# Reordering the first key chunks and splitting the query weight load at the start of a fused attention and feed-forward kernel

## The chip, the cores and the metric

The kernel runs on one core of one Trainium2 chip. The metric is device time in microseconds (us), and each number quoted for a kernel is the median of several runs. A profile's span is 1.2 to 1.4 us shorter than the time of the same run.

PE is TensorE's matmul, PEld its weight load, DVE is VectorE, ACT is ScalarE, and SP is SyncE, which here only issues transfers. ACT issues transfers too. "SPq" and "ACTq" are their issuing sequencers.

## The reference, cut to what matters

```python
def reference(A_x, A_wqkv, A_wo, B_x, B_w_gate, B_w_up, B_w_down, gate_w):
    x = A_x                                             # (1, 2048, 640), bf16
    g = sigmoid((x * gate_w).sum(-1, keepdims=True))
    # linear attention: q, k, v = x @ wqkv (640 -> 3 x 640), phi(q), phi(k), then @ wo
    a = _A_ref(x, A_wqkv, A_wo)
    b = (gelu(x @ w_gate) * (x @ w_up)) @ w_down        # 640 -> 1728 -> 640
    return g * a + (1 - g) * b
```

Only the start matters here: the key and query projections of the first two tiles of 128 rows of x. The contraction has length 640, so each projection is a sum of five chunks of 128 (k = 0 to 4).

Of the kernel before, what the change touches and what calls it, by code (L numbers as in the profile page):

```python
# [16 lines left out]
KC = D // 128  # L17
# [144 lines left out]
def bass_gated_mix__linear_attn_block__geglu_ffn__prompt_kernel(  # L162
# [63 lines left out]
    with (  # L226
# [8 lines left out]
        with contextlib.ExitStack() as stack:  # L235
# [12 lines left out]
            def new_dma_key():  # L248
                k = "in%d" % dma_next[0]
                dma_next[0] += 1  # L250
                return k
# [17 lines left out]
            wq = wkq[:, :, 640:1281]  # L269
# [40 lines left out]
            r_wq = [P.sb("wq%d" % k, R_WK + k * WW + 640, R_WK + k * WW + 1280) for k in range(KC)]  # L310
# [28 lines left out]
            def dma_in(dst, src, writes, reads=(), eng="sp"):  # L339
                P.op(eng, lambda e, dst=dst, src=src: e.dma_start(dst, src),  # L340
                     reads=reads, writes=writes, dma=new_dma_key())
# [6 lines left out]
            def load_wk(k, eng="sp"):  # L348
                dma_in(wk[:, k, :], A_wqkv[k * 128:(k + 1) * 128, 640:1280], [r_wk[k]], eng=eng)

            def load_wq(k0, k1, eng="sp"):
                dma_in(wq[:, k0:k1, 0:640],
                       A_wqkv[k0 * 128:k1 * 128, 0:640].rearrange("(k p) w -> p k w", p=128),
                       r_wq[k0:k1], eng=eng)


            P.op("act", lambda e: e.dma_start(touch[0:16, 0:4], A_wqkv[0:128:8, 640:644]),
# [10 lines left out]
            load_wk(4, "act")  # L368
            P.op("dve", lambda e: e.memset(gw_sb, 0.0), writes=[r_gw])
            dma_in(gw_sb[0:5, :], gate_w.rearrange("(k p) -> k p", p=128), [r_gw], eng="act")  # L370
            load_wq(0, 2)
            load_wq(2, KC, "act")

            def load_xT(i, after=()):
                P.op("sp", lambda e: e.dma_start_transpose(xT[:, :, i * 128:(i + 1) * 128],
# [50 lines left out]
            def slot(n):  # L426
                return SLOTS[n % 4]
# [17 lines left out]
            def KM(n, ks):  # L445
                i = seq[n][1]
                b0, b1 = slot(n)

                def fn(e):
                    last = None  # L450
                    for k in ks:
                        lhs = xT[:, k, i * 128:(i + 1) * 128]
                        e.matmul(ps[:, b0, :], lhs, wk[:, k, 0:512], start=(k == 0), stop=(k == KC - 1))  # L453
                        last = e.matmul(ps[:, b1, 0:128], lhs, wk[:, k, 512:640],
                                        start=(k == 0), stop=(k == KC - 1))
                    return last
                P.op("pe", fn, reads=[r_xTa[i] if i < NXN and ks == [0] else r_xT[i]] + [r_wk[k] for k in ks],
                     writes=[bank[b0], bank[b1]])

            def QM(n, ks):  # L460
                i = seq[n][1]
                b0, b1 = slot(n)

                def fn(e):
                    last = None
                    for k in ks:
                        lhs = xT[:, k, i * 128:(i + 1) * 128]
                        e.matmul(ps[:, b0, :], lhs, wq[:, k, 0:512], start=(k == 0), stop=(k == KC - 1))  # L468
                        last = e.matmul(ps[:, b1, 0:129], lhs, wq[:, k, 512:641],  # L469
                                        start=(k == 0), stop=(k == KC - 1))  # L470
                    return last
                P.op("pe", fn, reads=[r_xT[i], r_gcol] + [r_wq[k] for k in ks],
                     writes=[bank[b0], bank[b1]])

            def phi1(n):
                b0, b1 = slot(n)
                m = n % 4
                P.op("act", lambda e: e.activation(e_buf[m], ps_flat[:, b0 * 512:b0 * 512 + 640], ACT.Exp),
                     reads=[bank[b0], bank[b1]], writes=[r_e[m]])
                kind, i = seq[n]  # L480
                if kind == "q":
                    P.op("act", lambda e: e.activation(eg[:, i:i + 1], ps[:, b1, 128:129], ACT.Tanh, scale=0.5),
                         reads=[bank[b1]], writes=[r_eg[i]])

            def phi2(n):
                b0, b1 = slot(n)
                m = n % 4
                P.op("dve", lambda e: e.tensor_scalar(e_buf[m], e_buf[m], 1.0, EPS, ALU.min, ALU.add),
                     reads=[r_e[m]], writes=[r_e[m]])
                kind, i = seq[n]  # L490
                dst, r_dst = (pk[i], r_pk[i]) if kind == "k" else (pq[i], r_pq[i])
                P.op("dve", lambda e: e.scalar_tensor_tensor(
                    dst, ps_flat[:, b0 * 512:b0 * 512 + 640], 1.0 + EPS, e_buf[m], ALU.add, ALU.max),
                    reads=[bank[b0], bank[b1], r_e[m]], writes=[r_dst])

            def gate_col():

                P.op("pe", lambda e: e.matmul(ps[:, 7, 0:5], gw_sb, ident[:, 0:5], start=True, stop=True),
                     reads=[r_gw, r_ident], writes=[bank[7]])
                P.op("dve", lambda e: e.tensor_copy(wq[:, :, 640:641], ps[:, 7, 0:5].unsqueeze(2)),  # L500
                     reads=[bank[7]], writes=[r_gcol])
# [10 lines left out]
            T(1, [1, 2, 3, 4], 6)  # L512
            warm(3, 128)
            KM(1, [0])
            for k in (1, 3):
                KM(0, [k])
                KM(1, [k])
            gate_col()
            for k in (2, 4):
                KM(0, [k])  # L520
                KM(1, [k])
            for n in range(4):
                if n == 2:
                    for k in range(3):
                        QM(2, [k])
                        QM(3, [k])
                    QM(2, [3, 4])
                    QM(3, [3, 4])
                phi1(n)
                phi2(n)  # L530

# [398 lines left out]
```

## The kernel before: the parts that the change touches

The weights are loaded in pieces from two engines' queues. `dma_in(..., eng=...)` issues one load; whoever reads a piece waits for that load's own semaphore (a counter that the load's 16 shares raise one by one as they land: in the trace of this kernel those of key chunk 3 landed from 5.51 to 6.96 us, and the matmul that waited for it started at 7.01).

```python
load_x(0)                        # SP:  x tile 0, 160 KB
load_wk(0)                       # SP:  key weights, chunk 0, 160 KB
load_x(1, "act")                 # ACT: x tile 1
load_wk(1)
load_wk(3)                       # SP:  third key chunk on this queue
# [cut: one tiny activation]
load_wk(2, "act")
load_wk(4, "act")
# [cut: the gate vector, 1.2 KB, on ACT]
load_wq(0, 2)                    # SP:  query weights, chunks 0 and 1, one load of 320 KB
load_wq(2, KC, "act")            # ACT: query weights, chunks 2 to 4, one load of 480 KB
# [cut: 14 transposing loads of the other x tiles, which wait for key chunk 4; all later weights]
```

Tiles 0 and 1 are transposed on TensorE (`T`), with filler matmuls (`warm`) in the pauses. `KM(n, [k])` multiplies key chunk k of tile n (a matmul of 512 and one of 128 columns), `QM` does the same for queries (512 and 129 columns). `seq[2]` and `seq[3]` are the queries of tiles 0 and 1.

```python
warm(5, 512); warm(1, 128)
T(0, [0], 7); T(0, [1, 2, 3, 4], 6)
warm(6, 128)
KM(0, [0])
T(1, [0], 7); T(1, [1, 2, 3, 4], 6)
warm(3, 128)
KM(1, [0])
for k in (1, 3):
    KM(0, [k]); KM(1, [k])
gate_col()                       # one matmul of 5 columns
for k in (2, 4):
    KM(0, [k]); KM(1, [k])
for n in range(4):
    if n == 2:
        for k in range(3):
            QM(2, [k]); QM(3, [k])
        QM(2, [3, 4])
        QM(3, [3, 4])
    phi1(n); phi2(n)             # exponential on ACT, min and max on DVE
for i in range(2, NT):           # every other tile: keys and queries together, "joint tiles"
    KQ(i)                        # 15 matmuls, 2.7 us
```

After the joint tiles come the key-value products and the feed-forward block, another 220 us of matmuls.

## Time and profile before

| | before |
|---|---|
| time, median of 3 | 274.45 us (274.27 to 275.06) |
| span of the profile | 273.2 us |
| PE busy | 269.7 us (99%) |
| first key matmul | 4.62 us |
| first query matmul | 8.67 us |
| first joint tile | 11.40 us |

From the page of the kernel before, the span, the busy time of the engines, and the chain of work that ended last by engine:

```profile
span 273.2 us, 3449 instructions
PE 269.7 (99%) x1369; PEld 128.6 (47%) x1369; DVE 141.9 (52%) x251; ACT 76.0 (28%) x132; POOL 30.0 (11%) x28
...
PE 97%; DMA 2%; SPq 0%; DVE 0%; issue 0%
```

TensorE is nearly always busy and the chain is made of it. The list of PE's waits, for the whole run (engine, line, what it waited for, us in total, times, longest):

```profile
PE ps L419 <- PEq L915: 0.8, 1, 0.8
PE ps L453 <- DMA pool<-in_A_wqkv_dram: 0.8, 2, 0.6
```

So PE's only waits are the launch and 0.8 us for key weights (L453 is the key matmul). The chain in order of time (start, us, what) shows which load that was:

```profile
2.17 0.04 issue
2.21 4.76 DMA pool<-in_A_wqkv_dram
6.96 0.05 issue
7.01 0.39 PE ps L453
```

The load issued third on SP's queue, key chunk 3, ends at 6.96 and the next key matmul starts at 7.01. The timeline of PE (start, us, engine, line, operation, count, and the wait before it if one is listed) shows the gap; L453 and L454 are keys, L468 queries, L540 the joint tiles:

```profile
4.62 0.38 PE L453 MATMUL ps<-pool 128*128 128x512 bf16 x1 [0.18 <-DMA pool<-in_A_wqkv_dram]
...
6.20 0.22 PE L454 MATMUL ps<-pool 128*128 128x128 bf16 x1
7.01 0.39 PE L453 MATMUL ps<-pool 128*128 128x512 bf16 x1 [0.59 <-DMA pool<-in_A_wqkv_dram]
...
8.67 0.38 PE L468 MATMUL ps<-pool 128*128 128x512 bf16 x1
...
11.40 0.81 PE L540 MATMUL ps<-pool 128*128 128x512 bf16 x3
```

The listed time of a matmul is longer than the step to the next one: 0.38 us is listed for 512 columns and 0.22 for 128, but the next matmul starts 0.22 us after one of 512 columns and 0.05 after one of 128. From the start at 6.20 the next should have come at 6.26, so the gap is 0.75 us. The page's transfer list gives the two query loads: 320 KB took 5.9 us from issue to landing, 480 KB took 6.1. Issued at 2.68 and 3.32, they landed at about 8.5 and 9.4.

### The profile page before, as it was taken

The numbers are of one execution on the slowest core, as the hardware profiler recorded it, in microseconds if no ns is written. First come the engines' busy times: TensorE is split into PE (matmuls) and PEld (weight loads), VectorE is DVE, ScalarE is ACT, GpSimd is POOL, SyncE is SP. The second block draws the span as 40 slices with busy tenths as digits, with TensorE's granted clock in tenths as the row PEclk, the third lists the DMA queues.
The fourth block names the chain that finished last, engine by engine and source line by source line (L and its number), as shares of the span: only waits on it lengthen the run. The fifth ranks groups of instructions, "written<-read, shape, count | busy, mean of one in ns | idle before, by whom it ended". The sixth has DMA issues, their size and how long they took to land.

```text
span 273.2 us, 3449 instructions
## 1 busy us (share of the span) xinstructions
PE 269.7 (99%) x1369; PEld 128.6 (47%) x1369; DVE 141.9 (52%) x251; ACT 76.0 (28%) x132; POOL 30.0 (11%) x28
## 2 busy tenths in 40 slices
PE   7999999999999999999999999999999999999997
PEld 4555555544445444444444444444444444444444
DVE  2588989998234334999999999634210000000200
ACT  2355555310421454223222223224011121121021
POOL 5000000003240001242332422000000000000000
PEclk9999999999999999999999999999999999999999
DMA  6675999500300011522121221263031110110211
GB/s 207 179 118 122 322 402 386 143 3 12 65 19 2 23 49 51 182 45 48 26 48 24 48 42 34 60 215 109 5 77 38 41 38 19 38 41 19 58 58 41
DMA packets 42160, 23.61 MB, mean 86 GB/s; under 512 B 31519, under 2 KB 40735, under 8 KB 42015
## 3 DMA queue, kind: packets, MB, share of 16 engines
q1 hardware_dynamic: 41269, 22.40, 30.0%
q10 hardware_dynamic: 874, 0.98, 1.0%
q8 instruction: 11, 0.18, 0.3%
q14 instruction: 6, 0.05, 0.0%
HBM read 13.83 MB, written 2.63 MB: 60 GB/s over the span
## 4 chain that ended last, share of the span: by engine, by line
PE 97%; DMA 2%; SPq 0%; DVE 0%; issue 0%
PE ps L701 41%; PE ps L865 23%; PE ps L540 14%; PE ps L597 6%; PE ps L844 4%; DMA pool<-in_A_wqkv_dram 2%; PE ps L679 2%; PE ps L812 2%; PE ps L600 1%; PE ps L468 1%; PE ps L825 1%; PE ps L453 1%; PE ps L722 1%; PE ps L740 0%; SPq L340 0%; PE ps L469 0%
## 5 line engine op out<-in xcount | busy, mean ns | idle before, releaser
L701 PE MATMUL ps<-pool 128*128 128x512 bf16 x520 | 113.7, 379 | 0.0
L701 PEld LDWEIGHTS ps<-pool 128*128 128x128 bf16 x520 | 50.5, 98 | 60.0
L865 PE MATMUL ps<-pool 128*128 128x512 bf16 (+2 forms) x306 | 62.7, 367 | 0.0
L707 ACT ACTIVATE pool<-ps 128x512 f32<-128x512 f32 x52 | 31.0, 597 | 73.1 <-PE ps L701 73.1
L709 DVE TENSOR_TENSOR pool<-ps,pool 128x512 bf16<-128x512 f32 x52 | 34.7, 689 | 31.7 <-PE ps L701 30.4
L865 PEld LDWEIGHTS ps<-pool 128*128 128x128 bf16 x306 | 29.2, 98 | 33.4 <-issue 0.4
L540 PE MATMUL ps<-pool 128*128 128x512 bf16 (+1 forms) x210 | 38.1, 344 | 0.0
L848 DVE TENSOR_TENSOR pool<-ps,pool 128x512 bf16<-128x512 f32 x4 | 2.8, 692 | 61.5 <-PE ps L844 61.5
L755 POOL TENSOR_TENSOR pool<-pool 128x640 f32<-128x640 bf16 x16 | 22.5, 1406 | 72.9 <-DVE pool L757 66.2
L872 ACT ACTIVATE pool<-ps,pool 128x512 bf16<-128x512 f32 (+1 forms) x16 | 10.9, 681 | 68.6 <-PE ps L865 68.6
L540 PEld LDWEIGHTS ps<-pool 128*128 128x128 bf16 x210 | 20.5, 98 | 17.5
L559 DVE SCALAR_TENSOR_TENSOR pool<-ps,pool 128x128 bf16<-128x128 f32 (+2 forms) x42 | 25.3, 602 | 2.4
L550 ACT ACTIVATE pool<-ps 128x640 bf16<-128x640 f32 x28 | 19.7, 704 | 18.2 <-DVE pool L559 10.9
L597 PE MATMUL ps<-pool 128*128 128x512 bf16 x78 | 19.4, 379 | 0.0
L765 DVE TENSOR_TENSOR pool<-pool 128x640 bf16<-128x640 bf16 x16 | 13.2, 826 | 0.6
L763 DVE TENSOR_SCALAR pool<-pool 128x32 f32<-128x32 f32 x16 | 12.8, 802 | 0.6
L757 DVE TENSOR_REDUCE pool<-pool 128x32 f32<-128x640 f32 x16 | 12.9, 807 | 0.0
L645 DVE TENSOR_TENSOR pool<-pool 128x640 f32<-128x640 f32 x14 | 11.6, 825 | 0.5
L844 PE MATMUL ps<-pool 128*128 128x512 bf16 x52 | 11.6, 379 | 0.0
L647 POOL PARTITION_ALL_REDUCE pool<-pool x1 | 4.0, 3972 | 61.5 <-DVE pool L645 61.5
L597 PEld LDWEIGHTS ps<-pool 128*128 128x128 bf16 x78 | 7.0, 98 | 7.3
L556 DVE TENSOR_SCALAR pool<-pool 128x640 bf16<-128x640 bf16 x28 | 9.2, 327 | 1.8 <-ACT pool L550 0.3
(70 smaller groups left out, 105.8 us busy)
## 6 DMA issues: line engine op xcount, KB each, us to landing
out_dram<-pool SPq DMA_DIRECT2D x19, 128.0 KB, 1.7
pool<-in_B_w_gate_dram SPq DMA_DIRECT2D x1, 2080.0 KB, 13.8
pool<-in_B_w_up_dram SPq DMA_DIRECT2D x1, 2080.0 KB, 19.3
pool<-in_A_x_dram SPq DMA_DIRECT2D x1, 1280.0 KB, 8.6
pool<-in_B_w_down_dram SPq DMA_DIRECT2D x1, 1120.0 KB, 6.0
pool<-omg_row SPq DMA_DIRECT2D x1, 1024.0 KB, 4.8
pool<-in_A_x_dram SPq DMA_DIRECT2D x1, 960.0 KB, 5.7
pool<-in_A_wo_dram SPq DMA_DIRECT2D x6, 160.0 KB, 10.0
```

Source lines behind the costliest of these rows:

```text
L540: last = e.matmul(ps[:, b + p, 0:c1 - c0], xT[:, k, i * 128:(i + 1) * 128], wkq[:, k, c0:c1], start=(k == 0), stop=(k == KC - 1))
L550: P.op("act", lambda e: e.activation(e_buf[m], ps_flat[:, o:o + 640], ACT.Exp), reads=banks, writes=[r_e[m]])
L559: P.op("dve", lambda e, c0=c0, c1=c1: e.scalar_tensor_tensor(dst[:, c0:c1], ps_flat[:, o + c0:o + c1], 1.0 + EPS, e_buf[m][:, c0:c1], ALU. ...
L597: last = e.matmul(ps[:, b, :], pk[i][:, c * 128:(c + 1) * 128], x_aug[:, i, 0:512], start=(i == 0), stop=(i == NT - 1))
L701: last = e.matmul(ps[:, b, :], w[:, k, fc * 128:(fc + 1) * 128], xT[:, k, j * 512:(j + 1) * 512], start=(k == 0), stop=(k == KC - 1))
L707: P.op("act", lambda e: e.activation(ge[n], ps[:, gb, :], ACT.Gelu_apprx_tanh), reads=[bank[gb]], writes=[r_ge[n]])
L709: P.op("dve", lambda e: e.tensor_tensor(hT[fc][:, j * 512:(j + 1) * 512], ps[:, ub, :], ge[n], ALU.mult), reads=[bank[ub], r_ge[n]], write ...
L755: P.op("pool", lambda e: e.tensor_tensor(tmp[n], pq[i], z_b, ALU.mult), reads=[r_pq[i], r_zb], writes=[r_tmp[n]])
L757: P.op("dve", lambda e: e.tensor_reduce(den[n], tmp[n].rearrange("p (h d) -> p h d", h=32), AX.X, ALU.add), reads=[r_tmp[n]], writes=[r_de ...
L765: P.op("dve", lambda e: e.tensor_tensor(pq[i].rearrange("p (h d) -> p h d", h=32), pq[i].rearrange("p (h d) -> p h d", h=32), den[n].unsqu ...
L844: last = e.matmul(ps[:, b, :], wd[:, fc, 512:640], hT[fc][:, j * 512:(j + 1) * 512], start=False, stop=(fc == NFC - 2), skip_group_check=True)
L865: last = e.matmul(ps[:, pb, 0:c1 - c0], lhs, rhs, start=False, stop=(q == len(rows) - 1), skip_group_check=True)
```

## The change

The intent is to use key chunks in the order in which they land, and to make each query chunk a load of its own, so that the queries can start on chunk 0 as soon as it has landed. The queries of the two tiles are then interleaved to the end.

```diff
-            def load_wq(k0, k1, eng="sp"):
-                dma_in(wq[:, k0:k1, 0:640],
-                       A_wqkv[k0 * 128:k1 * 128, 0:640].rearrange("(k p) w -> p k w", p=128),
-                       r_wq[k0:k1], eng=eng)
+            def load_wq(k, eng="sp"):
+                dma_in(wq[:, k, 0:640], A_wqkv[k * 128:(k + 1) * 128, 0:640], [r_wq[k]], eng=eng)
@@
-            load_wq(0, 2)
-            load_wq(2, KC, "act")
+            for k in range(KC):
+                load_wq(k, ("sp", "act")[k % 2])
@@
-            for k in (1, 3):
+            for k in (1, 2, 3):
                 KM(0, [k])
                 KM(1, [k])
             gate_col()
-            for k in (2, 4):
+            for k in (4,):
                 KM(0, [k])
                 KM(1, [k])
             for n in range(4):
                 if n == 2:
-                    for k in range(3):
+                    for k in range(KC):
                         QM(2, [k])
                         QM(3, [k])
-                    QM(2, [3, 4])
-                    QM(3, [3, 4])
```

## The prediction

> **What bounds the kernel now.** TensorE: the busy table gives PE 269.7 of 273.2 us (99%), and the chain that ended last is 97% PE, 2% DMA. The list of waits shows none of PE after 11.4 us, and the granted clock is 1.00 throughout. So what lets PE begin its stream earlier moves the end by as much, and nothing else in this diff can matter. The diff touches only the first 11.4 us.
>
> **The first 11.4 us (timeline and chain).** PE multiplies key chunks 0 and 1 of both tiles until about 6.25 us, then sits until 7.01 for the load of key chunk 3 (in the chain: a DMA piece of 4.76 us that ends at 6.96). That is the only open gap of the stage, 0.75 us. Issue times plus times to landing give chunk 0 4.5, chunk 1 5.5, chunk 2 5.7, chunk 3 7.0, chunk 4 7.2 us. Order 0, 1, 3, 2, 4 thus waits for a late chunk while chunk 2 lies ready.
>
> **What the change does.**
> 1. Key order 0, 1, 2, 3, 4. One chunk of two tiles is four matmuls, 0.55 us (7.01 to 7.56). Chunk 2 now runs from 6.25 to 6.80, inside the gap; chunk 3 still waits until 7.01. The keys end near 8.1 instead of 8.65: 0.55 us off the chain, and a gap of 0.2 us stays.
> 2. Query loads. Before: 320 KB (landed 5.9 us after its issue, at 8.55) and 480 KB (at 9.4). The queries began at 8.67, barely after the first landing; with the new key order and old loads they would stall from 8.1 to 8.6, and most of the gain would be lost. Five loads of 160 KB complete one by one. Bytes are the same; three more issues cost about 0.4 us each on SP and ACT, which are idle then. [...] DMA busy share 0.98 from 3 to 7 us. So splitting adds no bandwidth, only earlier completion. My estimate from the packets: chunk 0 at 7.3 to 7.9, 1 at about 8.0, 2 and 3 at 8.5 to 9, 4 at 9.4. PE wants them at 8.1, 8.7, 9.2, 9.8, 10.3: all in time, chunk 0 and the gate column (written by DVE at 7.98) barely.
> 3. Queries chunk by chunk to the end: same matmuls. Tile 0's exponential comes 0.27 us later relative to PE; its banks are wanted over half a us after they are freed, so it costs nothing.
>
> **After that.** The next tile's transposed x landed at about 10.1 and is wanted at 10.85. Later tiles have more slack, and buffers are freed by work that PE itself triggers. The 0.55 us should reach the end.
>
> **Predicted time:** 273.9 us (274.45 minus 0.5), range 273.4 to 274.5, for the spread of single runs (274.27 to 275.06). Faster by over 2%: 0.5%; within 2%: 99%; slower by over 2%: 0.5%.
>
> **Right or wrong in the profile.** Right: the gap before the third key chunk shrinks from 0.75 to about 0.2 us, the first query matmul starts at 8.0 to 8.3 (was 8.67) without a DMA wait, the first joint tile at 10.8 to 11.0 (was 11.40), PE's busy total unchanged. Wrong: a DMA wait before a query chunk, a wait for the transposed x at 10.8, or waits after 11.4.
>
> **What would make it wrong.** Landings vary from run to run, so the gap may differ; the smaller loads could delay key chunks 3 or 4; query chunk 0 may land late; or a later stage waits for a load with an absolute time and gives the 0.5 us back.

## The result, and the profile after

The changed kernel took 273.55 us (median of 4 runs, 273.44 to 273.82) against 274.40 for the kernel before (4 runs). The ratio is 0.9969, with a 95% interval of 0.9955 to 0.9983. Ratios here are the mean time of one kernel's runs over that of the other's of the same rounds, so they are not quite the ratio of the medians.

From the page of the kernel after, the same three lines:

```profile
span 272.2 us, 3426 instructions
PE 267.9 (98%) x1343; PEld 128.1 (47%) x1369; DVE 141.8 (52%) x251; ACT 75.9 (28%) x132; POOL 30.0 (11%) x28
...
PE 95%; DVE 2%; DMA 1%; issue 1%; ACT 1%; SPq 0%; DVEq 0%; ACTq 0%
```

PE's busy time can't be compared here. The kernel has the same 1369 matmuls (there are 1369 weight loads), but this trace holds records of only 1343. The chain gained some DVE and ACT because it follows tile 0's exponential for a few us; PE lists no wait there. The list of PE's waits after:

```profile
PE ps L417 <- PEq L911: 0.8, 1, 0.8
PE ps L451 <- DMA pool<-in_A_wqkv_dram: 0.2, 1, 0.2
```

The timeline of PE after (L451 and L452 keys, L466 queries, L536 the joint tiles):

```profile
4.38 0.38 PE L451 MATMUL ps<-pool 128*128 128x512 bf16 x1 [0.21 <-DMA pool<-in_A_wqkv_dram]
...
6.28 0.38 PE L451 MATMUL ps<-pool 128*128 128x512 bf16 x1
6.50 0.22 PE L452 MATMUL ps<-pool 128*128 128x128 bf16 x1
6.55 0.38 PE L451 MATMUL ps<-pool 128*128 128x512 bf16 x1
...
7.67 0.38 PE L466 MATMUL ps<-pool 128*128 128x512 bf16 x1
...
10.39 9.80 PE L536 MATMUL ps<-pool 128*128 128x512 bf16 x51
```

The matmul at 6.55 is the first of key chunk 3, and there is no gap before it. The first joint tile starts 1.01 us earlier (10.39 against 11.40). The span shrank by 1.0 us. The 1.01 us has two parts:

- 0.24 us comes from before anything that the change touches: key chunk 0 landed at 4.24 instead of 4.49, so the first key matmul started at 4.38 instead of 4.62.
- 0.76 us is the gap before key chunk 3. Chunk 2 filled 0.55 of it, and the rest went because chunk 3 itself landed at 6.24 instead of 6.96.

These parts are not independent. With chunk 3 at 6.96 again, PE would have waited for it and the 0.24 us would have been lost in that wait. With chunk 3 at 6.24 and the old order, the gap would have been only about 0.28 us (an estimate: chunk 3 wanted at 6.01, started 0.05 after its landing), so how much of the 0.76 us is put down to the order depends on the landing.

Landing times in this document come from the trace's records of the loads' semaphores, and are those of the last of a load's 16 shares. The query chunks landed at 7.40, 7.84, 8.26, 8.96 and 8.92 us, each before PE asked for it.

So the result had more gain than the order of chunks explains, and the extra came from landings. That raised two questions. Did the smaller query loads make the key chunks land earlier, or was that chance? And how much of the change is real, when the start of the same kernel moves by tenths of a microsecond?

### The profile page after: what moved, and what is told of

Same layout as the page of the kernel before. It is cut to its first block, busy times and chain, and to the rows that moved or that the text cites. A ratio compares the mean times of both kernels' runs of the same rounds, so it can differ in the third digit from the quotient of the medians.

```text
span 272.2 us, 3426 instructions
## 1 busy us (share of the span) xinstructions
PE 267.9 (98%) x1343; PEld 128.1 (47%) x1369; DVE 141.8 (52%) x251; ACT 75.9 (28%) x132; POOL 30.0 (11%) x28
## 4 chain that ended last, share of the span: by engine, by line
PE 95%; DVE 2%; DMA 1%; issue 1%; ACT 1%; SPq 0%; DVEq 0%; ACTq 0%
PE ps L697 41%; PE ps L861 23%; PE ps L536 12%; PE ps L593 6%; PE ps L840 4%; PE ps L808 2%; PE ps L675 2%; PE ps L596 2%; DMA pool<-in_A_wqkv_dram 1%; PE ps L451 1%; PE ps L821 1%; PE ps L466 1%; DVE pool L490 1%; PE ps L718 1%; DVE pool L555 1%
## 5 line engine op out<-in xcount | busy, mean ns | idle before, releaser
L536 PE MATMUL ps<-pool 128*128 128x512 bf16 (+1 forms) x206 | 37.9, 344 | 0.2
L536 PEld LDWEIGHTS ps<-pool 128*128 128x128 bf16 x210 | 20.5, 98 | 17.5
```

Of the source, the lines that this page charges most:

```text
L536: last = e.matmul(ps[:, b + p, 0:c1 - c0], xT[:, k, i * 128:(i + 1) * 128], wkq[:, k, c0:c1], start=(k == 0), stop=(k == KC - 1))
```

## The experiments

Three theories were set up first. Theory A: the order fills the gap, the split loads only keep the queries from waiting in its place, and landings vary by chance. Rival B: the split loads bring the key chunks in earlier. Rival C: the order alone does it. Rival D came later: the gain is chance. Twelve runs were made, four at a time on one chip; all gave correct results.

### All traces in one table

The table is worked out from the traces' PE records. "Half speed until" is explained under before_again. "Lost to half speed" adds up, between the first key matmul and the first joint tile, by how much successive starts are further apart than at full speed. "Waits" are the other gaps in that stretch, without one of 0.09 us for a copy that most traces have. "Rest" is the span minus the start of the first joint tile. All times are in us.

| trace | first key matmul | half speed until | lost to half speed | waits | first joint tile | span | rest |
|---|---|---|---|---|---|---|---|
| before | 4.62 | 4.1 | 0 | 0.75 key 3 | 11.40 | 273.15 | 261.75 |
| before_again | 5.14 | 8.6 | 1.82 | none | 12.89 | 274.64 | 261.75 |
| inter_only | 4.61 | 3.7 | 0 | 0.24 key 3, 0.57 query 0 | 11.44 | 273.19 | 261.75 |
| order_only | 4.75 | 5.7 | 0.47 | 0.05 query 0 | 11.18 | 272.93 | 261.75 |
| loads_only | 4.32 | 5.7 | 0.71 | 0.41, 0.31 keys, 0.27 gate | 11.98 | 273.82 | 261.84 |
| loads_again | 4.72 | 5.2 | 0.21 | 0.21 key 1, 0.31 key 3 | 11.50 | 273.33 | 261.83 |
| after | 4.38 | 3.7 | 0 | none | 10.39 | 272.21 | 261.82 |
| after_again | 4.24 | 3.9 | 0 | 0.13 key 1 | 10.39 | 272.20 | 261.82 |
| after_third | 5.03 | 5.7 | 0.31 | none | 11.35 | 273.18 | 261.82 |
| after_fourth | 4.65 | 6.6 | 1.03 | none | 11.60 | 273.43 | 261.83 |
| split_first | 4.22 | 3.8 | 0 | 0.17, 0.13 keys, 0.21 query 2 | 10.77 | 272.52 | 261.75 |
| front | 4.75 | 7.2 | 1.26 | none | 11.93 | 273.76 | 261.83 |
| late3_old | 4.52 | 5.1 | 0.29 | 1.28 key 3 | 12.12 | 273.88 | 261.76 |
| late3_new | 5.05 | 6.1 | 0.54 | none | 11.52 | 273.27 | 261.75 |

The last column is the most useful: in 14 traces of nine kernels it stays within 0.09 us. All differences between these kernels, and between runs of one kernel, are made before the first joint tile, and they reach the end undiminished. (The kernels with five query loads have 0.07 us more. One weight load, 38.4 us after the first joint tile, starts 0.24 us later in them. Its cause was not looked into.)

### after_again, after_third, after_fourth: the changed kernel, three more times

The edit: none. Three jobs, on three chips.

> The changed kernel again, beside the kernel before on one chip. In the first pair of traces the first joint tile began 1.01 us earlier: 0.24 us because the first key chunk landed earlier (4.24 against 4.49), the rest because the gap before key chunk 3 went from 0.80 us (end of the last matmul's issue to the next) to none; chunk 3 landed at 6.24 instead of 6.96. Theory A (the order of the keys fills the gap, landings only vary from run to run): 0.5 to 0.9 us faster, chunk 3 lands anywhere between 6.2 and 7.0. Rival B (the split query loads make the key chunks land earlier): in this trace key chunk 3 is again near 6.2 and the first chunk near 4.25, while runs with the old loads show 6.9 and 4.5.

> The changed kernel a third time, for the spread of landings and for the moment TensorE's matmuls go to full speed. Theory A: first joint tile at 10.3 to 10.7 us in the trace, 0.5 to 0.9 us faster than before in the clocked runs. The first query chunk lands at 7.3 to 7.5 and no wait stands before the queries. In the two traces so far key chunk 3 landed at 6.24 and 6.23; Rival B (smaller query loads bring the key chunks in earlier) wants that again, theory A only wants it below 7.0.

> The changed kernel a fourth time. Its three jobs so far gave 0.85, 0.54 and 0.04 us less than before. Theory A with start noise: the sum of waits after the first key matmul is again below 0.2 us, and what varies is when the first key chunk lands (4.1 to 4.9 so far) and when the matmuls go from half to full speed (3.7 to 5.7 us); gain 0.0 to 0.9 us accordingly, late full speed going with a small gain. Rival D (the gain of the first job was chance, the change is worth nothing): waits of 0.6 us or more in the trace somewhere before the first joint tile.

Measured, against the kernel before on the same chip:

| | changed kernel | before | ratio, 95% interval |
|---|---|---|---|
| after_again | 273.99 (273.53 to 274.35) | 274.53 | 0.9978, 0.9949 to 1.0008 |
| after_third | 274.43 (274.31 to 274.63) | 274.47 | 0.9997, 0.9985 to 1.0009 |
| after_fourth | 274.50 (273.71 to 276.02) | 274.47 | 1.0007, 0.9984 to 1.0029 |

With the first job, the medians fell by 0.85, 0.54 and 0.04 us, and once rose by 0.03. In the traces the waits after the first key matmul were at most 0.13 us each time, so the change does what it was meant to, and rival D's waits of 0.6 us do not appear. Rival B gets no support in the sizes it needs: key chunk 3 landed at 6.23, 6.55 and 6.19 here, but also at 6.44, 6.41 and 6.49 in inter_only, order_only and before_again with the old query loads. The 6.96 of the first trace was late for the old loads too.

What took the gain away is seen in the timeline of PE in after_fourth:

```profile
4.65 0.58 PE L451 MATMUL ps<-pool 128*128 128x512 bf16 x1 [0.23 <-DMA pool<-in_A_wqkv_dram]
...
5.13 0.74 PE L431 MATMUL ps<-pool 128*128 128x128 bf16 x5
...
5.99 0.63 PE L451 MATMUL ps<-pool 128*128 128x512 bf16 x1
6.41 0.31 PE L452 MATMUL ps<-pool 128*128 128x128 bf16 x1
6.52 0.53 PE L451 MATMUL ps<-pool 128*128 128x512 bf16 x1
6.89 0.22 PE L452 MATMUL ps<-pool 128*128 128x128 bf16 x1
6.94 0.38 PE L451 MATMUL ps<-pool 128*128 128x512 bf16 x1
```

The key matmul of 512 columns takes 0.63 us at 5.99 and 0.38 at 6.94, with no wait listed. From one key step to the next it is 0.53 us (5.99 to 6.52) and from 6.94 on 0.27. In this run TensorE worked at half speed until about 6.6 us.

### before_again: the kernel before as if it were new

The edit: none.

> The kernel before, run as if it were a new one: the noise floor of the comparison, and a second trace of it. Expected ratio 1.000 plus or minus 0.001; in the trace a sum of waits after the first key matmul (before key chunks, or before the first query chunk) of 0.6 to 0.9 us, first joint tile at 11.2 to 11.6 us. If two loads of the same kernel differ by 0.5 us or more on one chip, differences of that size between kernels can't be read from one job.

Measured: 274.38 us (274.34 to 275.88), ratio 0.9999 (0.9987 to 1.0012). The comparison shows no bias of its own. But the trace is not what was expected: it is of the run of 275.88 us, and its first joint tile is at 12.89 us. The timeline of PE in before_again:

```profile
5.14 0.58 PE L453 MATMUL ps<-pool 128*128 128x512 bf16 x1 [0.62 <-DMA pool<-in_A_wqkv_dram]
...
7.01 0.63 PE L453 MATMUL ps<-pool 128*128 128x512 bf16 x1
7.44 0.31 PE L454 MATMUL ps<-pool 128*128 128x128 bf16 x1
...
8.51 0.31 PE L454 MATMUL ps<-pool 128*128 128x128 bf16 x1
8.61 0.54 PE L453 MATMUL ps<-pool 128*128 128x512 bf16 x1
8.99 0.22 PE L454 MATMUL ps<-pool 128*128 128x128 bf16 x1
...
12.89 0.38 PE L540 MATMUL ps<-pool 128*128 128x512 bf16 x1
```

TensorE works at half speed until 8.6 us, and chunks 1 to 4, landed at 5.85 to 6.75, are then never waited for. In such a run there is no gap for the change to fill. The two traces of this one kernel differ by 1.5 us, so, by the measure set above, differences of half a microsecond between kernels can't be read from one job. The view of stretches lists this one, from 5.00 to 8.60, with a granted clock of 1.00 (its columns: length, then each engine's busy time, then PEclk, DMA share and GB/s):

```profile
5.00:8.60 3.60, 3.46 (x18) 2.10 (x19) 0.65 (x2) 0.00 (x0) 0.00 (x0) 1.00 0.93 318
```

So that column does not show this half speed; only the matmuls' own times and spacing do. The traces show two speeds, one half of the other: 0.53 us per key step at half speed (6.48 to 7.01 in this trace), 0.27 at full speed. They show the change of speed at 3.7 to 8.6 us, though TensorE's first matmul is at 0.82 or 0.83 us in all 14. It came 2.9 us after that matmul in after and 4.9 us in loads_only, where no wait of PE is listed between the two, and 7.8 us after it in this trace, with a wait of 0.62 us listed before the first key matmul. It cost up to 1.82 us (here). What sets the moment was not tested.

### inter_only: one part of the change alone

```diff
-                    for k in range(3):
+                    for k in range(KC):
                         QM(2, [k])
                         QM(3, [k])
-                    QM(2, [3, 4])
-                    QM(3, [3, 4])
```

> Only the last two query chunks interleaved between the two tiles. All theories: no change, 0.0 plus or minus 0.2 us; tile 0's exponential begins 0.27 us later than before relative to the first joint tile's matmuls. If it is slower by 0.2 us or more, a later buffer wait was missed.

Measured: 274.38 us (274.24 to 276.25) against 274.53, ratio 0.9999 (0.9969 to 1.0029); the rest after the first joint tile is 261.75 us, as before. The interleaving is neutral. The trace also shows the second barrier of the old loads. The timeline of PE in inter_only:

```profile
6.19 0.22 PE L454 MATMUL ps<-pool 128*128 128x128 bf16 x1
6.49 0.39 PE L453 MATMUL ps<-pool 128*128 128x512 bf16 x1
...
8.10 0.22 PE L454 MATMUL ps<-pool 128*128 128x128 bf16 x1
8.72 0.38 PE L468 MATMUL ps<-pool 128*128 128x512 bf16 x1 [0.41 <-DMA pool<-in_A_wqkv_dram]
```

In this run key chunk 3 landed early (6.44), its gap was only 0.24 us and the keys were done half a microsecond sooner. The queries then waited for the 320 KB load, which landed at 8.59. The first query matmul came at 8.72, hardly different from the 8.67 of the first trace, which had a large key gap and no query wait.

### order_only: key order 0 to 4, query loads as before

```diff
-            for k in (1, 3):
+            for k in (1, 2, 3):
@@
-            for k in (2, 4):
+            for k in (4,):
```

> Key chunks in the order 0 to 4, query loads as before (320 and 480 KB), queries as before. Theory A: the keys end 0.55 us earlier, but the first query matmul waits for the 320 KB load, landed at about 8.5 before: a DMA wait ahead of the queries of 0.2 to 0.5 us, and a gain of only 0.1 to 0.4 us. Rival B: no gain or little, as key chunk 3 still lands at 6.9 (the gap is then 0.2 us and the gain up to 0.55 us less the query wait). Rival C (order is all, the split loads are needless): the full gain of 0.5 to 0.9 us and no DMA wait before the queries.

Measured: 274.18 us (274.02 to 274.34) against 274.53, ratio 0.998 (0.9954 to 1.0006). The trace had half speed until 5.7 us, which cost 0.47 us, so the keys ended at about 8.4, just after the 320 KB load (8.32), and the query wait was only 0.05 us, not the 0.2 to 0.5 expected. The five times are within 0.32 us of each other and none is below 274.02, while the whole change on the same chip reached 273.53. This fits a start held by the query load, but the trace does not show the wait itself at full speed; inter_only does.

### loads_only and loads_again: five query loads, key order as before

The edit is the diff of the change without its `for k in` lines of the keys and without the interleaving. It was run in two jobs.

> The five query loads on two queues, keys still in the order 0, 1, 3, 2, 4, last two query chunks still per tile. Theory A: no gain, 0.0 plus or minus 0.2 us; the gap before key chunk 3 stays, its size as chunk 3 happens to land. Rival B: key chunk 3 lands near 6.2 and the gap shrinks to about 0.1 us, gain 0.5 to 0.7 us, most of the gain of the whole change.

> The same kernel as loads_only, whose trace showed a late landing of all key chunks (chunk 1 at 6.39, 4 at 7.89) and slow matmuls until 5.7 us. If that was chance, the key chunks land as elsewhere (chunk 3 at 6.2 to 7.0), the queries begin without a wait 0.2 to 0.6 us earlier than in the kernel before where chunk 3 is early, and the time is 0 to 0.5 us below before. If the split loads with the old key order do harm of their own, it is again slower than before by about 0.6 us, with late key chunks again.

Measured: 275.16 us (274.13 to 276.23) against 274.53 in the first job, ratio 1.0012 (0.9983 to 1.0042); 274.48 (273.93 to 276.19) against 274.47 in the second, ratio 1.0004 (0.9984 to 1.0025). There is no gain in either, as theory A had it and against rival B. In both traces the key chunks landed late (chunk 3 at 7.26 and 7.06), the opposite of rival B, and PE waited for keys, 0.31 us of it for chunk 3 each time. The timeline of PE in loads_again (L451 and L452 are keys; the matmul at 7.11 is the first of chunk 3, due at 6.80):

```profile
6.75 0.22 PE L452 MATMUL ps<-pool 128*128 128x128 bf16 x1
7.11 0.39 PE L451 MATMUL ps<-pool 128*128 128x512 bf16 x1
```

In the second trace the first query matmul followed the keys without a wait. Up to key chunk 4 the loads and their issue times are those of the changed kernel to 0.01 us, and the first of chunk 3's 16 shares landed at 5.36 and 5.37, as early as in any trace with that load in its place; only the last ones were late. So the source of the kernel doesn't explain the late landings, and why they came in these two traces, and in none of the whole change, stays open. For the same reason the two traces don't show what the split loads alone do when the key chunks land early.

### split_first: only the first query load split

```diff
-            load_wq(0, 2)
+            load_wq(0, 1)
+            load_wq(1, 2)
             load_wq(2, KC, "act")
```

with the key order and the interleaving of the change.

> Key order 0 to 4 and queries chunk by chunk as in the change, but only the first query load split: chunks 0 and 1 as two loads on the first queue, chunks 2 to 4 still one load of 480 KB on the second. Refined theory A (what binds a query matmul is the landing of the last byte of its own load): no wait before query chunk 0 (lands 7.3 to 7.5), a wait of 0.3 to 0.6 us before chunk 2, because the 480 KB land at 9.0 to 9.4 and chunk 2 is wanted at 8.75. First joint tile 0.3 to 0.6 us later than the full change, about half of the gain. Rival C (the split is needless): no DMA wait at all, same time as the full change.

Measured: 274.09 us (273.86 to 275.12) against 274.47, ratio 0.999 (0.9976 to 1.0004). Query chunk 0 landed at 7.35 and was not waited for. The timeline of PE in split_first (L469 and L470 are queries):

```profile
8.65 0.38 PE L469 MATMUL ps<-pool 128*128 128x512 bf16 x1
8.87 0.22 PE L470 MATMUL ps<-pool 128*128 128x129 bf16 x1
9.13 0.39 PE L469 MATMUL ps<-pool 128*128 128x512 bf16 x1
```

The matmul at 9.13 is the first on chunk 2. It should have come at 8.92 and waited 0.21 us for the 480 KB load, landed at 9.08. The wait is where it was expected and somewhat smaller, because two key waits (0.17 and 0.13 us) had already delayed the queries. Here the matmul started 0.05 us after the last share of its whole load (9.13 and 9.08), so splitting one load moved the wait to the load that was left whole. This goes against rival C.

### late3_old and late3_new: the suspected wait made larger

Both move the load of key chunk 3 behind the 320 KB query load on SP's queue. The second also changes the order.

```diff
 # both
-            load_wk(3)
@@
             load_wq(0, 2)
+            load_wk(3)
 # late3_new only (and the closing flag of the sums moves from chunk 4 to chunk 3)
-            for k in (1, 3):
+            for k in (1, 2, 4):
@@
-            for k in (2, 4):
+            for k in (3,):
```

> The kernel before with the load of key chunk 3 moved behind the 320 KB query load on its queue, so that it surely lands last, at 8.0 to 8.8 us; key order 0, 1, 3, 2, 4 as before. TensorE must then wait for chunk 3 with three chunk steps (chunks 3, 2, 4) of 0.55 us still to do, so the keys end at about 10.1 and the first joint tile begins at about 12.9, whatever the start did. Expected about 1.4 us slower than before. The pair late3_old and late3_new doubles the suspected wait and takes the start out of the comparison.

> Same loads as late3_old, keys in the order of landing 0, 1, 2, 4, 3 (the closing flag moved to chunk 3). Theory A: two ready chunks, 1.1 us of matmuls, go into the wait; first joint tile 1.1 us earlier than in late3_old, and the time 0.9 to 1.2 us below it. If the order of ready chunks is not what matters (rivals B and D), it is the same as late3_old within 0.3 us.

Measured on one chip: late3_old 275.49 us (274.98 to 278.31), ratio to before 1.0066 (1.0027 to 1.0105); late3_new 274.16 us (273.74 to 277.00), ratio 1.0004 (0.9973 to 1.0036). The two medians are 1.33 us apart, more than the 0.9 to 1.2 expected. These figures include two runs of late3_old (278.24 and 278.31) and one of late3_new (277.00) that list a granted clock of 0.994. Without them the medians are 275.26 and 273.79, 1.47 us apart, and the runs of the two kernels do not overlap (274.98 to 275.59 against 273.74 to 274.60). The timeline of PE in late3_old:

```profile
6.39 0.22 PE L454 MATMUL ps<-pool 128*128 128x128 bf16 x1
7.73 0.39 PE L453 MATMUL ps<-pool 128*128 128x512 bf16 x1 [1.12 <-DMA pool<-in_A_wqkv_dram]
```

and the place where late3_new starts on chunk 3:

```profile
8.22 0.17 PE L498 MATMUL ps<-pool 128*128 128x5 bf16 x1
8.25 0.38 PE L453 MATMUL ps<-pool 128*128 128x512 bf16 x1
```

In late3_old the gap is 1.28 us (6.45 to 7.73; chunk 3 landed at 7.68, earlier than the 8.0 to 8.8 I had put down, so late3_old lost 1.0 us, or 0.8 without its two runs at 0.994, and not 1.4). In late3_new two ready chunks come first and chunk 3, landed at 7.61, is not waited for. Here the effect of using chunks in the order of landing is more than twice the 0.55 us of chunk 2 in the change, and stands out from the scatter.

The pair also shows another way to the same end. With the old, unsplit query loads, and only chunk 3 moved back and used last, three of six runs took 273.74 to 273.79 us, which would stand among the better half of the changed kernel's runs. The 320 KB load landed at 7.26 us there (6.96 in late3_old) instead of 8.27 to 8.59, because key chunk 3 no longer went ahead of it on its queue.

### front: a step further

```diff
-            P.op("act", lambda e: e.dma_start(touch[0:16, 0:4], A_wqkv[0:128:8, 640:644]),
-                 writes=[P.res("touch")], dma=new_dma_key())
             load_x(0)
-            load_wk(0)
+            load_wk(0, "act")
             load_x(1, "act")
@@
-            warm(6, 128)
+            warm(2, 128)
```

on the changed kernel.

> A step on from the change: the tiny load that opens the second queue is dropped, key chunk 0 is the second queue's first load (issued at about 0.8 instead of 1.26 us), every other load of the first queue moves up one place, and four of the six filler matmuls before the first key chunk go. In the changed kernel the first key matmul waited for this chunk (landed 4.1 to 4.2 in two traces). Expected: it lands at 3.4 to 3.8, first key matmul at 3.7 to 4.0, first joint tile 0.2 to 0.5 us earlier than the changed kernel on the same chip, if the later key chunks keep up. Rival: the total bandwidth before 6 us bounds it, chunks 3 and 4 become waits and nothing is gained; or the fewer fillers delay the moment of full matmul speed and it loses 0.3 us or more.

Measured: 274.94 us (274.66 to 276.42) against 274.47, ratio 1.0024 (1.0004 to 1.0043), slower. Key chunk 0 did land early, at 3.80. But x tile 0, which everything waits for first, landed at 3.98, where the other 13 traces have 2.97 to 3.13, and half speed lasted until 7.2 us. The timeline of PE in front (L429 is the transposing of x, L449 the keys):

```profile
4.03 0.71 PE L429 MATMUL ps<-pool 128*128 128x128 bf16 x5 [0.81 <-DMA pool<-in_A_x_dram]
...
6.67 0.63 PE L449 MATMUL ps<-pool 128*128 128x512 bf16 x1
```

The trace points to the key load beside it: from 1.5 to 3.0 us ACT's queue (key chunk 0 first) moved 0.15 MB and SP's (x tile 0 first) 0.11, where in the trace of the changed kernel SP's queue moved 0.23 MB and ACT's next to nothing. What the missing tiny load did was not separated, nor whether the pause of 0.8 us, the missing fillers or chance kept TensorE at half speed so long. No version that I tried was shown to beat the changed kernel.

## Why the prediction was right or wrong

The predicted time, 273.9 us in a range of 273.4 to 274.5, held the 273.55 us of the first job, and the class (within 2%) was right. That says little: the range also holds the 274.40 us of the kernel before, and of the 1.01 us in the first pair of traces only 0.55 had been forecast; the rest came from landings that differ from run to run, which is luck. Point by point:

- **"What lets PE begin its stream earlier moves the end by as much."** Right, and more exactly than I claimed: the rest after the first joint tile is 261.75 to 261.84 us in all 14 traces.
- **"0.55 us off the chain."** The mechanism was right: four matmuls of chunk 2 run in the gap, and late3_old and late3_new show the same with two chunks, at 1.28 us of wait removed.
- **"A gap of 0.2 us stays."** Wrong in size: no gap stayed in three of four traces of the change, and 0.13 us for another chunk in the fourth. I took chunk 3's landing at 6.96 us for a fixed time. In the other traces with its load in the same place it was 6.19 to 7.26. The load of key chunk 0 varied as much: in the 13 traces with the same issues ahead of it, it landed anywhere from 3.95 to 5.00 us. Within one load of 160 KB, key chunk 3, the shares landed 1.45 us apart in before (5.51 to 6.96) and 2.49 us apart in front.
- **"Query chunk by chunk [...] all in time."** Right. I put the landings at 7.3 to 7.9, 8.0, 8.5 to 9 twice and 9.4; they were 7.40, 7.84, 8.26, 8.96 and 8.92. Without the split the queries would wait: inter_only shows 0.57 us of it, split_first 0.21 us on the load left whole. From 3 to 7 us the two queues together filled the 16 DMA engines in both first traces: the packets of SP's queue took 56.0% of the engines' time and those of ACT's 42.4% before the change, 55.2% and 42.7% after it, and the DMA share is 0.98 in both.
- **"Costs nothing"** for the interleaving. Right: inter_only and split_first have the rest of the kernel before to 0.01 us.
- **First query matmul at 8.0 to 8.3 and first joint tile at 10.8 to 11.0.** It was 7.67 and 10.39. The 0.4 us beyond my figures are key chunk 0, 0.24 us earlier, and the 0.2 us gap that did not stay.
- **"The granted clock is 1.00 throughout."** This reading misled me. I took it to mean that the matmuls' pace at the start was given. It is the step of the prediction that would have failed in another job: at half speed until 6.6 us the changed kernel takes as long as the old one.

Over all jobs the changed kernel has a median of 274.23 us (20 runs) and the kernel before one of 274.47 (43 runs, before_again among them), so the gain is nearer 0.25 us than the 0.85 of the first job. These pools mix chips and are no paired comparison. Only the first job's interval lies wholly below 1, so the times alone do not show a gain over all starts; what the traces show is that the waits are gone. The fastest runs differ by 0.49 us (273.44 against 273.93). The traces suggest why the number is smaller. Of the kernel before, 34 of 43 runs lie between 274.20 and 274.69: with old loads, the queries can't start before the 320 KB load lands (8.27 to 8.59 us in its traces and those with its loads in place), and this hides a start that is late by half a microsecond. The changed kernel has removed that barrier and the key gap, so its time now follows how early key chunk 0 lands and how early TensorE reaches full speed. The two may be linked: of the 13 traces with key chunk 0 in its usual place, the six in which it landed at 4.51 us or later reached full speed at 5.2 us or later, and five of the other seven by 4.1. No run tests whether the pause before a late chunk delays full speed. In a good start it gains 0.5 to 0.9 us; in a late one, such as after_third, nothing.

What stays open: what sets the moment of full speed in one run, why the runs of some jobs agree (all five of after_third were slow starters by their times) and those of others don't (after_fourth, 273.71 to 276.02), and what made the key chunks late in loads_only and loads_again.

## What to carry to other kernels

Where an engine consumes pieces of loads in a fixed order, as TensorE did here (in before, key chunk 2 had landed at 5.68 us and was used at 7.59, after chunk 3), use them in the order of landing, and wait for each on its own; then look for the next barrier behind the one removed, since here two loads took turns at holding the start. Before you trust a gain of 0.3%, take several traces of both kernels, find the first point after which the rest is constant, and compare the times to that point part by part. At the start of a kernel, look at the duration of equal matmuls to see whether TensorE is at full speed (0.63 against 0.38 us for 512 columns in after_fourth).
